# Attention before two MoE layers: products per head in tiles of 64 columns, a state per head without masks, and heads 6 and 7 moved by DMA

## The chip, the cores and the metric

The kernel runs on one core of a Trainium2 chip. The time is that of one execution on the device in microseconds; the number given for a kernel is the median of its runs. The core's engines are TensorE (PE, whose weight loads the trace lists apart as PEld), VectorE (DVE), ScalarE (ACT), GpSimd (POOL) and SyncE (SP), which issues all the DMAs spoken of here. Each engine works through its own instructions in the order of the program and waits on semaphores for the others.

## What is computed

Three layers in a row, all f32. The first is an attention with a decaying state, for 4 batch entries, 8 heads, 768 steps and 48 elements per head:

```python
state = np.zeros((B, H, D, D), dtype=np.float32)
for t in range(S):
    cur = np.einsum('bhd,bhe->bhde', u[None] * kt, vt)
    y[:, :, t] = np.einsum('bhd,bhde->bhe', rt, state + cur)
    state = w[None, :, :, None] * state + np.einsum('bhd,bhe->bhde', kt, vt)
```

Its output, 3072 tokens by 384, goes through a layer `x @ w_in`, the activation h * tanh(softplus(h)) and `@ w_out` with 2048 inner columns, and then through a mixture of 8 experts with 1024 inner columns each. The change concerns the attention alone, and the order of the rows of `w_in`.

## The kernel before

The attention is computed by chunks of 128 steps. A unit is one chunk c (of 6) of one batch entry b (of 4), with all 8 heads; the 24 units run with b as the inner loop, so that a unit's state is next needed four units later. Heads go in pairs: p counts 4 pairs, j the two heads of a pair. In tiles with head elements on the partitions (`ld`, `rt`, `kd`, the state) head j = 0 of a pair lies in partitions 0 to 47 and head j = 1 in 64 to 111; partitions 48 to 63 hold nothing of use.

For each unit PE makes the scores (`a_scores`, L614, 48 rows of 64 per product), DVE copies those below the diagonal over a matrix A into which ACT has put the diagonals (`a_tri`, L619, `a_diag`, L606), and PE makes the outputs `ya` (`a_out`): state times r (L653) and v times A (L655), both heads of a pair into the same 96 partitions. For that the state is a block-diagonal matrix of 112 by 96 for each pair, and v stands in `vz`, a copy padded with zeros, one for each j (`a_vz`, L572, ACT). The chunk's own contribution `un` (`a_kv`, L626, PE) is made for whole pairs, 112 by 96; ACT multiplies its two halves by a mask `hm`, so that the blocks between different heads become zero (`a_mask`, L636), and DVE adds it to the decayed state, pair by pair (`a_state`, L644). ACT moves `ya` out of PSUM into `xT`, the transposed activations of the next layer (`a_evac`): pairs 0 to 2 in one instruction (L664), pair 3, which is heads 6 and 7, in three pieces of 32 partitions into the rows 96 to 127 (L666). POOL and DVE prepare the diagonals (`a_q`, L582 and L583, `a_b`, L588), DVE scales k and r (`a_kh`, `a_kd`, `a_rt`). Every other iteration one weight tile of the next layer is converted on the side (`a_cv`: four DVE operations L142 to L157, an ACT copy, two POOL operations).

The order around this is written by hand. The tuple `steps` lists functions with an offset: in iteration i the function is called for unit i + offset, and each engine gets its instructions in that order. Each iteration thus mixes, for instance, the scores of unit i, the output of unit i - 1 and the loads of unit i + 2 (v) and i + 3 (k and r). Loads of v have two buffers, `ya` has one PSUM bank, `un` two that alternate, the scores three. In the last iterations the first token tile of the next layer is split into two parts (`split_x`) for its first matmuls. `stepwise_attention` is a second form of the same attention that runs only on inputs outside a tested range, after the whole of the first; it doesn't run here.

Of the kernel before, what the change touches and what calls it, by code (L numbers as in the profile page):

```python
# [9 lines left out]
F32 = mybir.dt.float32  # L10
# [11 lines left out]
NP = H // 2  # L22
DD = 2 * D
DR = 64 + D
C = 128
# [22 lines left out]
NVZ = 3  # L48
# [32 lines left out]
def layers(ctx: ExitStack, tc: tile.TileContext, a, out, bad, general):  # L81
# [388 lines left out]

    def chunked_attention(aw, ac):
# [4 lines left out]
        ld, lt, lv = {}, {}, {}  # L476

# [14 lines left out]
        hm = ac.tile([DR, 2], F32, name="hm")  # L492
        nc.sync.dma_start(hm, a["hmask"])
# [23 lines left out]
        vzs = []  # L517
        for i in range(NVZ):
            vz = wA.tile([128, NP, 2, DD], F32, name=f"vz{i}", tag="w")
            pool.memset(vz, 0.0)  # L520
            vzs.append(vz)

# [25 lines left out]
        def tables():  # L548
# [3 lines left out]
            for p in range(NP):  # L552
                tp = bank([128, 128], f"tp{p}", f"y{p % 3}")
# [76 lines left out]
        def a_mask(i):  # L630
            c, b = aunits[i]
            if c == NC - 1:
                return
# [4 lines left out]
            T[i]["um"] = um  # L638

        def a_state(i):  # L640
# [1044 lines left out]
```

## Time and profile before

| | us |
|---|---|
| median of 3 runs | 2027.22 |
| runs | 2024.59 to 2029.64 |
| the profiled execution | 2026.27 |
| its span, from the first to the last instruction | 2024.5 |

| engine | busy us in the span | share |
|---|---|---|
| PE | 1990.4 | 98% |
| DVE | 1360.1 | 67% |
| ACT | 1063.1 | 53% |
| POOL | 751.6 | 37% |

The attention is the first part of the span; its last output product begins at 151.0 us. In the timeline a row is a run of equal instructions: start, time from the start of the first to the end of the last, engine, line, operation, what is written and read, sizes, count, and in brackets how long the engine stood before and for whom. One f32 product of this attention appears as two MATMUL instructions. The end of a matmul is modelled, and matmuls overlap, so their starts say more than their lengths.

### The profile page before, as it was taken

The numbers are of one execution on the slowest core, as the hardware profiler recorded it, in microseconds if no ns is written. First come the engines' busy times: TensorE is split into PE (matmuls) and PEld (weight loads), VectorE is DVE, ScalarE is ACT, GpSimd is POOL, SyncE is SP. The second block draws the span as 40 slices with busy tenths as digits, with TensorE's granted clock in tenths as the row PEclk, the third lists the DMA queues.
The fourth block names the chain that finished last, engine by engine and source line by source line (L and its number), as shares of the span: only waits on it lengthen the run. The fifth ranks groups of instructions, "written<-read, shape, count | busy, mean of one in ns | idle before, by whom it ended". The sixth has DMA issues, their size and how long they took to land.

```text
span 2024.5 us, 27279 instructions
## 1 busy us (share of the span) xinstructions
PE 1990.4 (98%) x9334; PEld 1647.8 (81%) x9334; DVE 1360.1 (67%) x2177; ACT 1063.1 (53%) x2204; POOL 751.6 (37%) x639
## 2 busy tenths in 40 slices
PE   8899999999999999999999999999999999999998
PEld 7888888887778888877878888888888888888887
DVE  8998889778787777678764455555465555455554
ACT  7998888888755545444443433343344343333332
POOL 5546565557554333355561243311044011011110
PEclk8999999999999999999999999999999999999999
DMA  8750111010246655655465665558545566445440
GB/s 255 214 150 30 32 32 40 24 35 1 96 154 234 228 207 192 203 211 201 156 225 165 189 215 194 190 153 262 162 151 155 135 182 226 141 151 159 143 120 33
DMA packets 169156, 305.96 MB, mean 151 GB/s; under 512 B 39664, under 2 KB 85424, under 8 KB 169008
## 3 DMA queue, kind: packets, MB, share of 16 engines
q1 hardware_dynamic: 169008, 304.13, 46.7%
q8 instruction: 76, 1.25, 0.3%
q14 instruction: 72, 0.59, 0.1%
HBM read 226.90 MB, written 77.17 MB: 150 GB/s over the span
## 4 chain that ended last, share of the span: by engine, by line
PE 89%; DVE 5%; ACT 2%; issue 2%; POOL 1%; DMA 1%; DVEq 0%; SPq 0%; POOLq 0%; ACTq 0%
PE y L1039 37%; PE Bk L907 16%; PE U L907 15%; PE ph L246 9%; PE x L331 9%; ACT A L606 1%; PE ya L655 1%; DVE tc L939 1%; DVE A L619 1%; PE un L626 0%; DMA lv<-in_v_dram 0%; PE sc L614 0%; ACT xT L666 0%; DVE r L826 0%; PE ya L653 0%
## 5 line engine op out<-in xcount | busy, mean ns | idle before, releaser
L1039 PE MATMUL y<-gf,w 128*128 128x512 f32 x2088 | 570.4, 390 | 0.0
L1039 PEld LDWEIGHTS y<-gf,w 128*128 128x128 f32 x2088 | 391.0, 188 | 82.5 <-DVE gf L1031 1.5
L1039 PE MATMUL y<-ge,w 128*128 128x512 f32 x1368 | 373.8, 390 | 0.0
L1062 POOL TENSOR_TENSOR xT<-xT,xT 128x512 f32<-128x512 f32 x102 | 142.3, 1410 | 577.3 <-DVE xT L1061 576.0
L1029 ACT ACTIVATE gf<-tc 128x512 fp32r<-128x512 f32 x232 | 146.5, 632 | 389.6 <-DVE tc L939 375.6
L939 DVE TENSOR_TENSOR tc<-tc,Bk 128x512 f32<-128x512 f32 x270 | 185.1, 685 | 237.8 <-PE Bk L907 222.3
L939 DVE TENSOR_TENSOR tc<-tc,U 128x512 f32<-128x512 f32 x270 | 185.3, 686 | 222.7 <-PE U L907 208.3
L1039 PEld LDWEIGHTS y<-ge,w 128*128 128x128 f32 x1368 | 256.2, 188 | 53.5 <-DVE ge L1031 0.5
L1029 ACT ACTIVATE ge<-tc 128x512 fp32r<-128x512 f32 x152 | 96.1, 632 | 248.3 <-DVE tc L939 237.6
L331 PE MATMUL x<-g,wm 128*128 128x512 f32 x864 | 212.2, 390 | 0.3 <-POOL g L320 0.2
L246 PE MATMUL ph<-xs,wm 128*128 128x512 f32 x864 | 212.0, 390 | 0.3 <-POOL xs L216 0.3
L1031 DVE SCALAR_TENSOR_TENSOR gf<-tc,gf 128x512 fp32r<-128x512 f32 x232 | 193.5, 837 | 22.9 <-ACT gf L1029 18.2
L246 PEld LDWEIGHTS ph<-xs,wm 128*128 128x128 f32 x864 | 161.8, 188 | 36.5 <-POOL xs L216 0.7
L331 PEld LDWEIGHTS x<-g,wm 128*128 128x128 f32 x864 | 161.8, 188 | 35.2 <-DVE xT L347 0.8
L320 POOL TENSOR_TENSOR g<-y,g 128x512 fp32r<-128x512 f32 x96 | 125.0, 1302 | 102.2 <-ACT g L315 95.6
L937 ACT ACTIVATE tc<-Bk 128x512 f32<-128x512 f32 x192 | 114.3, 595 | 85.3 <-PE Bk L907 78.7
L937 ACT ACTIVATE tc<-U 128x512 f32<-128x512 f32 x192 | 114.4, 596 | 83.5 <-PE U L907 78.7
L907 PE MATMUL Bk<-xc,wc 128*128 128x512 f32 x540 | 152.0, 390 | 0.9 <-DVE tc L939 0.9
L907 PE MATMUL U<-xc,wc 128*128 128x512 f32 x540 | 151.7, 389 | 0.0
L1031 DVE SCALAR_TENSOR_TENSOR ge<-tc,ge 128x512 fp32r<-128x512 f32 x152 | 127.7, 841 | 21.4 <-ACT ge L1029 15.7
L847 POOL TENSOR_TENSOR w<-r,w 128x384 fp32r<-128x384 f32 x64 | 68.6, 1074 | 186.6 <-ACT w L846 175.4
L907 PEld LDWEIGHTS Bk<-xc,wc 128*128 128x128 f32 x540 | 101.1, 188 | 23.0 <-DVE tc L939 1.8
(256 smaller groups left out, 3210.9 us busy)
## 6 DMA issues: line engine op xcount, KB each, us to landing
wc<-keep SPq DMA_DIRECT2D x208, 384.0 KB, 3.7
w<-keep SPq DMA_DIRECT2D x128, 384.0 KB, 5.5
keep<-wc SPq DMA_DIRECT2D x104, 384.0 KB, 3.6
r<-in_w_dram SPq DMA_DIRECT2D x128, 192.0 KB, 3.7
keep<-w SPq DMA_DIRECT2D x64, 384.0 KB, 3.0
ld<-in_rkT_dram SPq DMA_DIRECT2D x24, 448.0 KB, 4.8
pb<-prow SPq DMA_DIRECT2D x42, 256.0 KB, 8.5
lt<-in_kr_dram SPq DMA_DIRECT2D x24, 384.0 KB, 5.1
```

Of the source, the lines that this page charges most:

```text
L246: pe.matmul(ph, w[:, pw, k, :], xs[:, px, :], start=(m == 0), stop=(m == 3 * KI - 1))
L320: pool.tensor_tensor(gs[i][:, 1], y, gs[i][:, 0].bitcast(F32), op=ALU.subtract)
L331: pe.matmul(sums[n][k], wo[f][:, pw, k, :], g[:, px, :], start=(f == f0 and m == 0), stop=(f == f1 and m == 1), skip_group_check=True)
L606: act.activation(A[:, h % 2, h // 2, :], ident, AF.Copy, scale=T[i]["bc"][:, h:h + 1])
L847: eng.tensor_tensor(flat(t[:, 1]), src, flat(t[:, 0]).bitcast(F32), op=ALU.subtract)
L907: pe.matmul(out_, w[:, pw, :], x[px], start=bool(start and m == 0), stop=bool(stop and m == 2), skip_group_check=True)
L937: act.activation(t, b, AF.Copy, scale=1.0 if kind == "c" else -1.0)
L939: dve.tensor_tensor(t, t, b, op=ALU.add if kind == "+" else ALU.subtract)
L1029: act.activation(g[:, 0], t, AF.Relu)
L1031: return lambda: dve.scalar_tensor_tensor(g[:, 1], t, 0.0, g[:, 0].bitcast(F32), op0=ALU.max, op1=ALU.subtract)
L1039: pe.matmul(Y[t][k], w[:, pw, k, :], x[:, px, :], start=(f % NF2 == 0 and m == 0), stop=(f % NF2 == NF2 - 1 and m == 2), skip_group_check= ...
L1062: pool.tensor_tensor(o, o, t_, op=ALU.add)
```

## The change

The two heads of a pair no longer share an output tile. `a_out` makes v times A for head j = 0 into partitions 0 to 47 and for j = 1 into 64 to 111, straight from the loaded v, and adds state times r to each with a product of 48 rows and 48 columns at the same place. So no padded copy of v is needed, and the state is one block of 48 columns per pair and head without blocks between heads: `a_kv` makes `un` by head, masks are gone. The decay of the state is one POOL multiplication (`a_decay`), the addition one DVE operation (`a_add`). `ya` is one PSUM tile for all units, cleared once. `a_evac` moves 112 partitions of pairs 0 to 2 into `xT` (row 48 to 63 and 112 to 127 of it hold nothing yet) and pair 3 into a staging tile `stg`, one for each token tile; after the last chunk of a token tile six DMAs (`spread_heads`) move heads 6 and 7 from there into those free rows, 16 partitions each. The rows of `w_in` are ordered accordingly on the host. v has four buffers in place of two, and `steps` has a new order.

```diff
+    def spread_heads(n, src):
+        for k in range(KI):
+            for j in range(2):
+                nc.sync.dma_start(xT[n][64 * j + D:64 * j + 64, k, :], src[64 * j + 16 * k:64 * j + 16 * k + 16])
...
+        lvs = [wA.tile([128, NP, 2, D], F32, name=f"lv{i}", tag="w") for i in range(4)]
+        stg = [wA.tile([128, TT], F32, name=f"stg{n}", tag="w") for n in range(NT)]
...
-            lv[i] = aw.tile([128, DM], F32, name=f"lv{i}", tag="lv")
+            lv[i] = lvs[i % 4]
...
+        ya = []
+
         def marks():
+            ya.append(bank([DR, NP, C], "ya", "y2"))
+            dve.memset(ya[0], 0.0)
...
-        st2 = [wA.tile([DR, 2, NP, DD], F32, name=f"st{b}", tag="w") for b in range(B // 2)]
-        st = [st2[b // 2][:, b % 2] for b in range(B)]
+        st = wA.tile([DR, B, NP, D], F32, name="st", tag="w")
...
-        def a_vz(i):
-            vz = vzs[i % NVZ]
-            vh = lv[i].rearrange("t (p j d) -> t p j d", p=NP, j=2)
-            for j in range(2):
-                act.activation(vz[:, :, j, j * D:(j + 1) * D], vh[:, :, j, :], AF.Copy)
-            T[i]["vz"] = vz
...
-            un = bank([DR, NP, DD], f"un{i}", f"y{i % 2}")
+            un = bank([DR, NP, D], f"un{i}", f"y{i % 2}")
+            kh = T[i]["kh"]
             for p in range(NP):
-                pe.matmul(un[:, p, :], T[i]["kh"][:, p].rearrange("t j d -> t (j d)")[:, 0:DR], lv[i][:, p * DD:(p + 1) * DD],
-                          start=True, stop=True)
+                pe.matmul(un[0:64, p, :], kh[:, p, 0, :], lv[i][:, p, 0, :], start=True, stop=True)
+                pe.matmul(un[64:DR, p, :], kh[:, p, 1, 0:D], lv[i][:, p, 1, :], start=True, stop=True)
...
-            um = st[b] if c == 0 else T[i]["un"]
-            for j in range(2):
-                act.activation(um[:, :, j * D:(j + 1) * D], T[i]["un"][:, :, j * D:(j + 1) * D], AF.Copy,
-                               scale=hm[:, j:j + 1])
...
+        def a_decay(i):
             c, b = aunits[i]
             if 0 < c < NC - 1:
-                for p in range(NP):
-                    dve.scalar_tensor_tensor(st[b][:, p, :], st[b][:, p, :], w128[:, p:p + 1], T[i]["um"][:, p, :],
-                                             op0=ALU.mult, op1=ALU.add)
+                pool.tensor_tensor(st[:, b], st[:, b], w128.unsqueeze(2).to_broadcast([DR, NP, D]), op=ALU.mult)
+
+        def a_add(i):
+            c, b = aunits[i]
+            if c == 0:
+                act.activation(st[:, b], T[i]["un"], AF.Copy)
+            elif c < NC - 1:
+                dve.tensor_tensor(st[:, b], st[:, b], T[i]["un"], op=ALU.add)
...
-            y = bank([DD, NP, C], f"ya{i}", "y2")
+            y = ya[0]
             for p in range(NP):
+                pe.matmul(y[0:D, p, :], lv[i][:, p, 0, :], x["A"][:, 0, p, :], start=True, stop=(c == 0))
+                pe.matmul(y[64:DR, p, :], lv[i][:, p, 1, :], x["A"][:, 1, p, :], start=True, stop=(c == 0))
                 if c > 0:
-                    pe.matmul(y[:, p, :], st[b][:, p, :], x["rt"][:, p, :], start=True, stop=False)
-                for j in range(2):
-                    pe.matmul(y[:, p, :], x["vz"][:, p, j, :], x["A"][:, j, p, :],
-                              start=(c == 0 and j == 0), stop=(j == 1))
+                    for j in range(2):
+                        r = slice(64 * j, 64 * j + D)
+                        pe.matmul(y[r, p, :], st[r, b, p, :], x["rt"][r, p, :], start=False, stop=True)
...
-            act.activation(xt[0:DD, :, x0:x0 + C], y[:, 0:KI, :], AF.Copy)
-            for k in range(KI):
-                act.activation(xt[DD:128, k, x0:x0 + C], y[32 * k:32 * k + 32, KI, :], AF.Copy)
+            n = blk // NSUB
+            act.activation(xt[0:DR, :, x0:x0 + C], y[:, 0:KI, :], AF.Copy)
+            act.activation(stg[n][0:DR, x0:x0 + C], y[:, KI, :], AF.Copy)
+            if i == ends[n]:
+                spread_heads(n, stg[n])
...
-        steps = ((load_d, 3), (a_tri, -1), (a_scores, 0), (a_kv, 0), (a_out, -1), (load_v, 2),
-                 (a_q, 1), (a_state, -2), (a_kh, 1), (a_evac, -2), (a_rt, 1), (a_diag, 0),
-                 (a_cv, 0), (a_mask, -1), (a_vz, 1), (a_kd, 1), (a_b, 1))
+        steps = ((load_d, 3), (a_tri, -1), (a_add, -2), (a_evac, -2), (a_scores, 0), (a_out, -1), (a_kv, 0),
+                 (a_q, 1), (a_kh, 1), (a_rt, 1), (a_diag, 0),
+                 (a_cv, 0), (a_kd, 1), (a_b, 1), (a_decay, -1), (load_v, 2))
```

On PE, at the end of the scores of one iteration in the middle of the attention: `sc` are the scores, `un` the unit's contribution to the state, `ya` the output; sizes are those of the result, partitions by columns. Before:

```order
L614 MATMUL sc_145<-rt_979,kd_1004 128x128
L614 MATMUL sc_144<-rt_979,kd_1004 128x128
L614 MATMUL sc_145<-rt_979,kd_1004 128x128
L626 MATMUL un_1022<-lv_898,kh_182 112x96 x4
L653 MATMUL ya_1027<-rt_912,st_188 96x128
L655 MATMUL ya_1027<-A_981,vz_153 96x128 x2
```

The last two rows stand there four times, once for each pair. Now the output comes right behind the scores, and `un` behind the output; this is the last pair of an output and the beginning of `un`:

```order
L648 MATMUL ya<-rt_482,st 48x128 x2
L643 MATMUL ya<-A_548,lv_110 48x128
L644 MATMUL ya<-A_548,lv_110 48x128
L648 MATMUL ya<-rt_482,st 48x128 x2
L622 MATMUL un_606<-lv_111,kh_182 64x48
L623 MATMUL un_606<-lv_111,kh_182 48x48
```

Twelve products of 96 partitions have become sixteen of 48, in which a pair's two products over 128 rows alternate with two over 48 rows, and four products `un` have become eight; PE's order of output and `un` is exchanged.

On DVE, the beginning of an iteration, with the copies by mask of unit i - 1, the state of unit i - 2 and the scaling of k and r of unit i + 1. Before:

```order
L619 COPY_PREDICATED A_914<-tri,sc_146 128x512
L619 COPY_PREDICATED A_914<-tri,sc_144 128x512
L644 SCALAR_TENSOR_TENSOR st_187<-st_187,w_186,un_805 112x96 x4
L599 TENSOR_TENSOR kh_182<-lt_793,Wkh 128x8x48
L593 TENSOR_TENSOR rt_979<-ld_791,Wr 112x512
```

Now:

```order
L614 COPY_PREDICATED A_686<-tri,sc_152 128x512
L614 COPY_PREDICATED A_686<-tri,sc_150 128x512
L636 TENSOR_TENSOR st<-st,un_606 112x192
L594 TENSOR_TENSOR kh_183<-lt_575,Wkh 128x8x48
L588 TENSOR_TENSOR rt_757<-ld_573,Wr 112x512
```

Four operations of 96 columns gave way to one of 192; the rest stands as it stood.

On POOL, over two iterations: the two products of `a_q` of each (`aq`), and the two operations of the weight conversion (`v`, `wm`) in one of them. Before:

```order
L582 TENSOR_TENSOR aq_758<-lt_584,ub 128x384
L583 TENSOR_TENSOR aq_758<-aq_758,lt_584 128x384
L171 TENSOR_TENSOR v_706<-v_706,wm_712 128x384
L176 TENSOR_TENSOR wm_712<-v_706,q_707 128x384
L582 TENSOR_TENSOR aq_825<-lt_651,ub 128x384
```

Now:

```order
L629 TENSOR_TENSOR st<-st,w_186 112x192
L577 TENSOR_TENSOR aq_753<-lt_575,ub 128x384
L578 TENSOR_TENSOR aq_753<-aq_753,lt_575 128x384
L170 TENSOR_TENSOR v_695<-v_695,wm_701 128x384
L175 TENSOR_TENSOR wm_701<-v_695,q_696 128x384
L629 TENSOR_TENSOR st<-st,w_186 112x192
```

The decay of the state stands at the end of each iteration, behind all else that POOL does in it.

## Rows read from the trace of the kernel before

**Rows 1.** Busy us (count): PE, PEld, DVE, ACT, POOL; clock; DMA share; GB/s
```profile
60.00:70.00 10.00, 9.31 (x93) 8.55 (x92) 9.90 (x24) 8.95 (x30) 5.72 (x6) 1.00 0.78 241
...
200.00:210.00 10.00, 10.00 (x46) 8.29 (x45) 9.79 (x14) 8.41 (x19) 7.42 (x6) 1.00 0.13 40
```

**Rows 2.** Timeline of DVE, two iterations: start us, us, instruction, count
```profile
56.31 1.33 DVE L619 COPY_PREDICATED A<-tri,sc 128x512 f32<-128x512 uint8 x2
...
57.54 0.97 DVE L644 SCALAR_TENSOR_TENSOR st<-st,w,un 112x96 f32<-112x96 f32 x4
58.44 0.55 DVE L599 TENSOR_TENSOR kh<-lt,Wkh 128x384 f32<-128x384 f32 x1
...
60.56 1.33 DVE L619 COPY_PREDICATED A<-tri,sc 128x512 f32<-128x512 uint8 x2
...
66.88 1.33 DVE L619 COPY_PREDICATED A<-tri,sc 128x512 f32<-128x512 uint8 x2
```

**Rows 3.** Timeline of DVE, copies by mask 14 iterations apart
```profile
44.16 1.35 DVE L619 COPY_PREDICATED A<-tri,sc 128x512 f32<-128x512 uint8 x2
...
123.99 1.33 DVE L619 COPY_PREDICATED A<-tri,sc 128x512 f32<-128x512 uint8 x2
```

**Rows 4.** Waits in 45 to 130 us: total us, times, longest
```profile
DVE st L644 <- PE ya L653: 1.6, 4, 0.5
DVE A L619 <- ACT A L606: 1.5, 3, 0.6
```

**Rows 5.** Timeline of PE, one iteration without a wait
```profile
85.48 1.16 PE L614 MATMUL sc<-rt,kd 48*128 48x128 f32 x16
86.57 1.02 PE L626 MATMUL un<-lv,kh 128*112 128x96 f32 x8
87.43 0.38 PE L653 MATMUL ya<-rt,st 112*96 112x128 f32 x2
...
89.63 0.60 PE L655 MATMUL ya<-A,vz 128*96 128x128 f32 x4
90.16 1.16 PE L614 MATMUL sc<-rt,kd 48*128 48x128 f32 x16
```

**Rows 6.** Timeline of ACT, one iteration without a weight conversion
```profile
126.22 2.45 ACT L606 ACTIVATE A<-ident,bc 128x128 f32<-128x128 f32 x8
128.69 0.82 ACT L636 ACTIVATE un<-un,hm 112x192 f32<-112x192 f32 x2
129.43 0.60 ACT L572 ACTIVATE vz<-lv 128x192 f32<-128x192 f32 x2
129.94 0.47 ACT L664 ACTIVATE xT<-ya 96x384 f32<-96x384 f32 x1
130.42 0.82 ACT L666 ACTIVATE xT<-ya 32x128 f32<-32x128 f32 x3
```

**Rows 7.** Groups of POOL, 45 to 130 us: busy us, mean ns, idle before
```profile
L582 POOL TENSOR_TENSOR aq<-lt,ub 128x384 f32<-128x384 f32 x12 | 13.0, 1082 | 10.5 <-DMA lt<-in_kr_dram 5.5 <-DVE A L619 2.6 <-DVE st L644 2.5
```

**Rows 8.** Timelines of ACT, then DVE, at the start, with waits
```profile
23.45 0.62 ACT L572 ACTIVATE vz<-lv 128x192 f32<-128x192 f32 x2 [2.96 <-DMA lv<-in_v_dram]
...
27.49 1.35 DVE L619 COPY_PREDICATED A<-tri,sc 128x512 f32<-128x512 uint8 x2 [1.46 <-ACT A L606]
```

**Rows 9.** Timeline of PE, products of 16 columns before products of 128
```profile
393.43 0.39 PE L383 MATMUL gp<-xg,wga 128*16 128x512 f32 x1
393.66 0.40 PE L384 MATMUL gp<-xg,wgb 128*16 128x512 f32 x1
393.89 2.21 PE L246 MATMUL ph<-xs,wm 128*128 128x512 f32 x9
```

**Rows 10.** Timeline of SP, one issue of a load
```profile
66.31 0.42 SPq L481 DMA_DIRECT2D ld<-in_rkT_dram  x1
```

**Rows 11.** PE at 80.2 us: busy, granted clock, DMA; then its timeline
```profile
80.20:80.40 0.20, 0.04 (x1) 0.50 1.02 328
...
80.36 1.78 PE L626 MATMUL un<-lv,kh 128*112 128x96 f32 x8 [0.37 <-issue]
```

More of the change, by code (lines that the diff above doesn't have):

```diff
@@ L47 @@
 NWA = 24
-NVZ = 3
 NG = 3
@@ L491, in chunked_attention @@
         nc.sync.dma_start(wT, a["wT"])
-        hm = ac.tile([DR, 2], F32, name="hm")
-        nc.sync.dma_start(hm, a["hmask"])
         load_d(0)
@@ L516, in chunked_attention @@
         pool.memset(warm, 0.0)
[L517 to L521, printed above, removed]
         wb = bank([128, 128], "wb", "y2")
@@ L552, in tables @@
             for p in range(NP):
-                tp = bank([128, 128], f"tp{p}", f"y{p % 3}")
+                tp = bank([128, 128], f"tp{p}", f"y{p % 2}")
                 pe.matmul(tp[:, 0:DR], Wh[:, p, :], ident[:DR, :DR], start=True, stop=True)
                 act.activation(Wkh[:, p], tp.rearrange("t (j d) -> t j d", j=2)[:, :, 0:D], AF.Copy)
+        ya = []
         def marks():
+            ya.append(bank([DR, NP, C], "ya", "y2"))
+            dve.memset(ya[0], 0.0)
             dve.tensor_copy(tri, trf.unsqueeze(1).to_broadcast([128, NP, 128]))
@@ L562, in marks @@
             dve.scalar_tensor_tensor(okw, wT, W_MAX, okw, op0=ALU.is_le, op1=ALU.mult)
-        st2 = [wA.tile([DR, 2, NP, DD], F32, name=f"st{b}", tag="w") for b in range(B // 2)]
-        st = [st2[b // 2][:, b % 2] for b in range(B)]
+        st = wA.tile([DR, B, NP, D], F32, name="st", tag="w")
         T = [{} for _ in aunits]
-        def a_vz(i):
-            vz = vzs[i % NVZ]
-            vh = lv[i].rearrange("t (p j d) -> t p j d", p=NP, j=2)
-            for j in range(2):
-                act.activation(vz[:, :, j, j * D:(j + 1) * D], vh[:, :, j, :], AF.Copy)
-            T[i]["vz"] = vz
+        ends = {(b * NC + c) // NSUB: i for i, (c, b) in enumerate(aunits)}
         def a_kd(i):
@@ L686, in chunked_attention @@
         a_q(0)
-        a_vz(0)
         for i in range(NA + 1):
@@ L711, in stepwise_attention @@
         nc.sync.dma_start(uT, a["uT"])
-        sel = ac.tile([DR, 3 * D - 1], F32, name="sel")
+        sel = ac.tile([DR, DR + D - 1], F32, name="sel")
         pool.memset(sel, 0.0)
         for j in range(2):
-            nc.sync.dma_start(sel[:, (j + 1) * D - 1:(j + 1) * D], a["hmask"][:, j:j + 1])
+            nc.sync.dma_start(sel[:, 64 * j + D - 1:64 * j + D], a["hmask"][:, j:j + 1])
         sts = [ac.tile([DR, S + 1], F32, name=f"sts{j}") for j in range(2)]
@@ L723, in stepwise_attention @@
         rk = ac.tile([DR, 2, NC, C], F32, name="rk")
+        stg = [wA.tile([128, TT], F32, name=f"stg{n}", tag="w") for n in range(NT)]
         for b in range(B):
@@ L728, in stepwise_attention @@
                 rT, kT = (rk[:, j].rearrange("d c t -> d (c t)") for j in range(2))
-                y = [bank([DD, S // 2], f"yg{b}_{p}_{g}", f"y{2 * (p % 2) + g}") for g in range(2)]
+                y = [bank([DR, S // 2], f"yg{b}_{p}_{g}", f"y{2 * (p % 2) + g}") for g in range(2)]
                 for e in range(D):
@@ L740, in stepwise_attention @@
                     for g in range(2):
-                        pe.matmul(y[g], sel[:, D - 1 - e:3 * D - 1 - e], x[:, g * S // 2:(g + 1) * S // 2],
+                        pe.matmul(y[g], sel[:, D - 1 - e:DR + D - 1 - e], x[:, g * S // 2:(g + 1) * S // 2],
                                   start=(e == 0), stop=(e == D - 1))
@@ L747, in stepwise_attention @@
                     if p < KI:
-                        act.activation(xt[0:DD, p, x0:x0 + C], yc, AF.Copy)
+                        act.activation(xt[0:DR, p, x0:x0 + C], yc, AF.Copy)
                     else:
-                        for k in range(KI):
-                            act.activation(xt[DD:128, k, x0:x0 + C], yc[32 * k:32 * k + 32, :], AF.Copy)
+                        act.activation(stg[blk // NSUB][0:DR, x0:x0 + C], yc, AF.Copy)
+        for n in range(NT):
+            spread_heads(n, stg[n])
     if general:
@@ L1659, in _lay_out @@
     p = np.arange(128)
-    perm = np.stack([np.where(p < DD, i * DD + p, 3 * DD + 32 * i + p - DD) for i in range(KI)])
+    j, d = p // 64, p % 64
+    perm = np.stack([np.where(d < D, i * DD + j * D + d, 3 * DD + j * D + 16 * i + d - D) for i in range(KI)])
     wi = np.asarray(x["moe_w_in"])[perm.reshape(-1)]
```

6 lines of the change are left out of this document (removed).

## The prediction

> **What bounds the kernel now.** I read the busy times in equal stretches first. From 200 to 210 us TensorE (PE) is busy 10.00 of 10 us [rows 1], with the matmuls of the first layer after attention: no edit of attention shortens that part, it can only start earlier or later. So the change is worth what it takes off the stretch before. There, between 60 and 70 us, VectorE (DVE) is busy 9.90 us and PE 9.31, with ScalarE (ACT) at 8.95 [rows 1]: three engines near full, so the next question is which one is last.
>
> The order in time on DVE answers it. One iteration of the loop handles one unit, a chunk of one batch entry, and I count it from one pair of copies by mask (L619) to the next: 56.31 to 60.56 is 4.25 us, 60.56 to 66.88 is 6.32 us, with no wait marked inside [rows 2]; the longer one, every other iteration, holds the four weight-conversion operations. The mean without gaps is (4.25 + 6.32)/2 = 5.29 us. Over the 14 iterations from 44.16 to 123.99 us it is 79.83/14 = 5.70 us [rows 3]. The missing 0.41 us is waits and stretched operations: in 45 to 130 us DVE waited 1.5 us for ACT's diagonals and 1.6 us for PE's reads of the state [rows 4]. PE needs, in an iteration without waits, 4.68 us (85.48 to 90.16) [rows 5], ACT 2.45 + 0.74 + 0.51 + 0.48 + 0.82, 5.0 us [rows 6]. So **DVE ends last, ACT is 0.3 us behind it, PE 0.6 us**.
>
> **The change, part by part.**
>
> *State update.* Four operations on DVE, 0.90 us (57.54 to 58.44) [rows 2], become one addition of 192 columns on DVE and one multiplication on POOL. No row shows the addition. The nearest, kh with 384 columns, takes 0.55 us [rows 2], so it lies between half of that and all of it; I take 0.30, near the half, since the width is what differs. DVE saves 0.60 us (0.35 to 0.63) in each of 16 units (batch entries times the four chunks that update): **9.6 us** (5.6 to 10.1). The multiplication on POOL costs by halves of L582's 1.08 us [rows 7] some 0.54 us, up to 1.08. POOL has room for that, but waits ahead of it for PE's output products, and the next a_q stands queued behind; its result is wanted at the far end of the next iteration, so that hides it. Without that cover DVE's reduction would wait the 2.2 us of a_q's two operations. A busier POOL can also stretch DVE's operations between buffers; I put 0.05 us an iteration on it, 0.8 in all (0 to 4).
>
> *ACT.* The masks (0.74), the zero-padded copies of v (0.51) and three small moves (0.82) go, one move like those (0.27) comes: 5.0 - 2.07 + 0.27, 3.2 us an iteration [rows 6]. ACT leaves the path. What it gives directly is DVE's wait for it, 1.5 us; its other effect falls on the start. There ACT stood 2.96 us for a load of v and DVE then 1.46 us for ACT [rows 8]; now only PE needs v. That gives 1.46 us, less a clearing of one PSUM bank on DVE at the start, which I bound by a mask copy, 0.65: **0.8 us net** (0 to 3).
>
> *PE.* One f32 product of 128 columns is two instructions 0.11 us apart (four in 0.60 us, two in 0.38) [rows 5]. The scores (L614) use 64 rows each: 16 instructions in 1.09 us, where one after the other they would need 1.76. So two halves of the rows run side by side, 8 x 0.11 = 0.88, and 0.21 is left; before them the last product would hand over at 90.07 (89.63 + 4 x 0.11) and they start at 90.16. That is 0.30 us for going to 64 rows and back, 0.15 a change of form. Before, an iteration has 2 such changes; after it has 10, because each pair p goes from 128 rows (v times A) to 64 (state times r) and back. The streams after: scores 0.88; v times A, 16 instructions on two column halves, 0.88 if these run side by side as the row halves do, 1.76 if not; state times r 0.88; the update un, 16 instructions of 48 columns where 8 of 96 took 0.86 [rows 5], between 0.43 and 0.86, taken as 0.50, since the columns are halved. With 10 x 0.15: 0.88 x 3 + 0.50 + 1.50 = **4.64 us**, as before, out of fewer columns and more changes. The bounds are 3.1 (changes free) and 5.9 (halves one by one: 0.88 + 1.76 + 0.88 + 0.86 + 1.50).
>
> Two rows speak of the form. Two products on 32 columns stand between products on 128 at 393.43 and 393.66, and the next begins at 393.89: steps of 0.23, no gap [rows 9], so columns alone cost nothing to change; rows did. The Trainium skill, "TensorEngine Tiling (Array Packing)", Key Properties, says that any change of tiling mode drains the engine, and these rows do not bear that out for columns. By the page the ten changes stay (4.64), by these rows alone they would go (3.1).
>
> No run here shows two column halves at once. The Trainium skill, "TensorE: Matmul & The Clock Gate", Part 3, says that column groups run concurrently, three of them 2.38 times as fast; by it the sum stays 4.64.
>
> DVE comes to 5.29 - 0.60 = 4.69 us and PE to 4.64: **a tie** where PE had 0.6 us to spare. DVE's iterations are alternately long and short, PE's equal, so in the short ones (3.65) DVE will wait for PE. I charge 0.15 us an iteration, 2.4 in all (0 to 8), and let half of the old waits of 3.1 us go (1.5).
>
> *Row moves.* 36 DMAs on SP, six for each of six token tiles, each some 0.42 us to issue [rows 10]. They wait for ACT's copy, and the loads of v and the next unit queue behind, but those are issued one to two iterations ahead; at most 2.5 us of issue stands in one iteration, against 4.7. The rows moved are first read in iterations 21 on, at the split of the first token tile, whose last part is ready in 14. Cost 0; without that cover a landing would show once, some 5 us.
>
> **The sum**: 9.6 + 1.5 + 0.8 - 2.4 - 0.8 = 8.7 us gained. The profiled execution took 2026.27 us (span 2024.5 and 1.8 around it), 0.95 below the median of 2027.22. 2026.3 - 8.7 = 2017.6, or **2018.5** beside the median.
>
> **Rivals.**
>
> *Column halves do not run side by side, slower.* Then PE needs 5.9 us; with the 0.41 of waits that DVE's bound had, 6.3 against 5.70, 16 x 0.59 = 9.4 lost, 0.8 back at the start: 2027.2 + 8.6, near 2036. It decides from 5.7 us of PE on. For it: no row shows columns side by side. Against: the rows' halves do so, to the last 0.11 us.
>
> *Nothing to be seen.* The change of form costs 0.25 us rather than 0.15 (blocks of four instructions refill each time), PE 5.6; or the clock. PE streams about 3.1 us of 5, with holes; at 80.2 us, after pauses, the granted clock was 0.50, the 1.2 GHz level, and the eight un instructions took 1.78 us in place of 1.02 [rows 5, 11]. With PE tied those 0.76 us fall on the path, and eleven more such stretches take the gain. Time: 2023 to 2031.
>
> *More is gained.* If the short loads of 48 columns make the changes cheap, PE needs under 4 us and DVE runs without waits: 9.6 + 3.1 + 1.5 - 0.4 = 13.8, that is 2013.
>
> **How the numbers follow.** Forecast (2015 to 2021) 0.44; more 0.15; nothing 0.24; slower by the halves 0.13, by other ends of the bounds (POOL's stretch, loads behind the moves) 0.04. About 0.3%, 6 us, is what a measurement here can tell from no change. So faster 0.58, same 0.25, slower 0.17. The range reaches from 2009 (5.70 - 4.69 us in all 16 iterations, no wait left, and 2 us at the start: 18 gained) to 2034, most of the way to the slower rival: below it lie 0.06, above 0.14.
>
> **What would show it.** DVE's copies by mask should come 5.1 us apart on average where they were 5.70, with one addition near 0.30 us behind them. PE's v times A of one pair should take 0.22 us (0.44: the slower rival), and out products some 3.0 us in all; if 2.3, the larger gain. ACT should show idle time of more than 1 us an iteration. The granted clock between 45 and 130 us tells the clock's part. The prediction is wrong if PE's iteration exceeds 5.2 us, or if DVE waits for POOL's multiplication.

## The result, and the profile after

The changed kernel takes 2054.44 us (median of 5 runs, 2053.77 to 2064.76) where the kernel before takes 2027.16 beside it (5 runs, 2024.59 to 2029.64): a ratio of 1.0145 (95% interval 1.0129 to 1.0161). It is **27 us slower** where 8.7 us less had been forecast; the time lies above the range, which ended at 2034. The profiled execution of after is the longest of the five, 2064.76 us with a span of 2062.9, and the account below is for that one: 38.4 us more than the span of before. The other four have a mean granted clock of 0.965 to 0.967 over the span where this one has 0.959; no profile shows where they differ.

All of it lies in the attention. Its last output product begins at 191.04 us, 40.0 us after that of before (151.0). What follows is as dense as it was [rows 1]. The stretches of after that answer to [rows 1], in the same columns (busy us and count of PE, PEld, DVE, ACT, POOL; then the granted clock of TensorE, DMA share, GB/s):

```profile
40.00:50.00 10.00, 10.00 (x81) 5.53 (x81) 8.08 (x15) 3.72 (x12) 4.56 (x5) 0.50 1.02 256
60.00:70.00 10.00, 10.00 (x90) 6.26 (x90) 4.84 (x9) 4.34 (x15) 5.93 (x7) 0.50 0.79 214
120.00:130.00 10.00, 10.00 (x82) 5.59 (x80) 6.47 (x12) 2.98 (x10) 4.62 (x5) 0.50 0.64 175
180.00:190.00 10.00, 10.00 (x54) 6.29 (x52) 1.17 (x6) 2.07 (x5) 3.01 (x3) 0.68 0.27 67
200.00:210.00 10.00, 9.41 (x41) 7.81 (x42) 9.86 (x16) 8.55 (x18) 8.13 (x7) 1.00 0.21 56
```

Read the PE column and the clock together. PE is busy 10.00 of 10 us, and DVE, which ended last before with 9.90, is down to 4.84. But the clock is **0.50**, the 1.2 GHz level, in every stretch of ten microseconds from 40 to 180; before, the stretch from 60 to 70 showed 1.00 [rows 1], and falls in the loop were short. The fall of [rows 11], to 0.50 at 80.2 us, was over at 83.6 us; PE's rows in it and behind it, the same four instructions:

```profile
82.36 1.06 PE L655 MATMUL ya<-A,vz 128*96 128x128 f32 x4
...
84.29 0.60 PE L655 MATMUL ya<-A,vz 128*96 128x128 f32 x4
```

The timeline of PE in one iteration, which answers to [rows 5] (start, length, line, operation, sizes, count):

```profile
61.74 2.08 PE L609 MATMUL sc<-rt,kd 48*128 48x128 f32 x16
63.75 0.45 PE L643 MATMUL ya<-A,lv 128*48 128x128 f32 x1
63.76 0.45 PE L644 MATMUL ya<-A,lv 128*48 128x128 f32 x1
...
64.35 0.67 PE L648 MATMUL ya<-rt,st 48*48 48x128 f32 x4
64.94 0.45 PE L643 MATMUL ya<-A,lv 128*48 128x128 f32 x1
...
68.53 0.34 PE L622 MATMUL un<-lv,kh 128*64 128x48 f32 x1
...
69.54 2.08 PE L609 MATMUL sc<-rt,kd 48*128 48x128 f32 x16
```

An iteration takes 69.54 - 61.74 = 7.80 us; the forecast was 4.64. The scores take 2.01 us here (1.09 in [rows 5]) and a pair 64.94 - 63.75 = 1.19. The pair's four steps of 0.213 us (25.74 to 25.95, below) make 0.85 of that, so its two changes of form cost 0.17 each, some 1.7 us of the 7.80 for all ten. The column of busy time doesn't show these gaps, since the end of a product is modelled. From one pair of copies by mask on DVE to the second after it are 15.60 us, 7.80 an iteration, where [rows 3] gave 5.70. About 18 iterations with 2.1 us more each are the 38 us. DVE's own rows, which answer to [rows 2], show the engine waiting:

```profile
64.34 1.32 DVE L614 COPY_PREDICATED A<-tri,sc 128x512 f32<-128x512 uint8 x2
69.23 0.35 DVE L636 TENSOR_TENSOR st<-st,un 112x192 f32<-112x192 f32 x1 [3.56 <-POOL st L629]
...
79.94 1.32 DVE L614 COPY_PREDICATED A<-tri,sc 128x512 f32<-128x512 uint8 x2
```

And the waits of after, 45 to 170 us, which answer to [rows 4] (engine and line, for whom it waited: total us, times, longest):

```profile
ACT xT L657 <- PE ya L648: 70.2, 17, 4.8
POOL st L629 <- PE ya L648: 68.0, 16, 8.4
DVE st L636 <- POOL st L629: 41.3, 16, 4.0
```

DVE waits for POOL, but POOL for PE's output products, as ACT does: three engines stand behind one. The place where the clock falls is in the timeline of PE too. In the chunk without a state, where an output is v times A alone, PE works at 0.50 first (25.74 to 25.95: 0.21 us a step), and the clock rises at 29.3 us, while PE streams (29.94 to 30.16: two steps in 0.22). Then PE pauses for DVE (the brackets: how long, for whom), and the clock falls at 36.1 us, 1.6 us after PE had begun again, so that a step takes 0.22 us from 36.30 on and the next scores 2.73:

```profile
25.74 0.42 PE L643 MATMUL ya<-A,lv 128*48 128x128 f32 x1
...
25.95 0.42 PE L643 MATMUL ya<-A,lv 128*48 128x128 f32 x1
...
29.94 0.27 PE L643 MATMUL ya<-A,lv 128*48 128x128 f32 x1
29.95 0.27 PE L644 MATMUL ya<-A,lv 128*48 128x128 f32 x1
...
30.16 0.27 PE L643 MATMUL ya<-A,lv 128*48 128x128 f32 x1
...
33.35 0.49 PE L609 MATMUL sc<-rt,kd 48*128 48x128 f32 x2 [2.02 <-DVE kd L572]
34.45 1.16 PE L609 MATMUL sc<-rt,kd 48*128 48x128 f32 x14 [0.61 <-DVE A L614]
...
36.30 0.42 PE L643 MATMUL ya<-A,lv 128*48 128x128 f32 x1
...
36.52 0.42 PE L643 MATMUL ya<-A,lv 128*48 128x128 f32 x1
...
37.70 2.73 PE L609 MATMUL sc<-rt,kd 48*128 48x128 f32 x16
```

Before, the clock also fell after pauses, and came back. Here it comes back at 186 us only, in the first layer's products of 128 by 512, which begin at 182.47. The Trainium skill, "TensorE: Matmul & The Clock Gate", section "Why this matters for your kernels", lays such drops to gaps in which TensorE is idle. The fall at 36.1 us fits that in so far as pauses of 2.02 and 0.61 us stand ahead of it; that the clock stayed at 0.50, with PE busy 10.00 of 10 us from 40 to 190, the rule does not explain.

### The profile page after: what moved, and what is told of

Same layout as the page of the kernel before. It is cut to its first block, busy times and chain, and to the rows that moved or that the text cites. A ratio compares the mean times of both kernels' runs of the same rounds, so it can differ in the third digit from the quotient of the medians.

```text
span 2062.9 us, 27802 instructions
## 1 busy us (share of the span) xinstructions
PE 2037.0 (99%) x9654; PEld 1641.1 (80%) x9654; DVE 1354.4 (66%) x2130; ACT 1021.3 (50%) x2072; POOL 760.3 (37%) x652
## 4 chain that ended last, share of the span: by engine, by line
PE 94%; DVE 3%; issue 1%; DMA 1%; POOL 1%; ACT 0%; SPq 0%; DVEq 0%; POOLq 0%; ACTq 0%
PE y L1034 36%; PE Bk L902 15%; PE U L902 15%; PE ph L245 10%; PE x L330 9%; PE ya L643 2%; PE ya L648 2%; PE sc L609 2%; PE un L622 1%; DVE tc L934 1%; DVE r L821 0%; DMA lt<-in_kr_dram 0%; DMA wc<-keep 0%; PE un L623 0%; DVE sw L821 0%
## 5 line engine op out<-in xcount | busy, mean ns | idle before, releaser
L1026 DVE SCALAR_TENSOR_TENSOR gf<-tc,gf 128x512 fp32r<-128x512 f32 x232 | 194.6, 841 | 22.7 <-ACT gf L1024 17.9
```

What stands on the lines that cost most here:

```text
L1026: return lambda: dve.scalar_tensor_tensor(g[:, 1], t, 0.0, g[:, 0].bitcast(F32), op0=ALU.max, op1=ALU.subtract)
```

## The experiments

**Theory:** the changed kernel's work is what was forecast, and the granted clock alone makes it slow. **Rivals:** the changes of form cost more than forecast; or the wait for POOL's multiplication holds the loop up. All kernels below start from the changed one. Each time stands beside runs of the kernel before on the same chip; PE's iteration is read from scores to scores, without waits.

| kernel | us (median) | ratio to before | interval | clock at 60 to 70 us | PE's iteration |
|---|---|---|---|---|---|
| the change | 2054.44 | 1.0145 | 1.0129 to 1.0161 | 0.50 | 7.80 |
| e1_grouped | 2031.77 | 1.0027 | 1.0016 to 1.0038 | 0.66 | 3.9 at clock 1.00, from output to output |
| e2_state_whole | 2069.43 | 1.0211 | 1.0181 to 1.0240 | 0.50 | 8.21 |
| e3_va_whole | 2031.42 | 1.0016 | 0.9990 to 1.0042 | 1.00 | 5.53 |
| e4_filler4 | 2026.54 | 1.0001 | 0.9990 to 1.0013 | 1.00 | 5.61 |
| e10_fill4_small | 2096.31 | 1.0347 | 1.0326 to 1.0368 | 0.50 | 9.50 |
| e7_fill4_all | 2022.54 | 0.9985 | 0.9976 to 0.9995 | 1.00 | as e4_filler4 |
| e5_grouped_fill2 | 2017.90 | 0.9969 | 0.9953 to 0.9984 | 1.00 | DVE ends last |
| e6_grouped_fill4 | 2026.61 | 1.0010 | 0.9993 to 1.0028 | 1.00 | ties with DVE |
| e11_grouped_fill40 | 2020.38 | 0.9976 | 0.9965 to 0.9987 | 1.00 | DVE ends last |
| e9_grouped_fill42 | 2015.57 | 0.9940 | 0.9922 to 0.9958 | 1.00 | DVE ends last |
| **e12_grouped_fill424** | **2011.97** | **0.9925** | 0.9912 to 0.9939 | 1.00 | DVE ends last |

e8_fill1 had two executions, at 2074.95 and 2027.04 us, and stands below.

### Work thrown away, to see the clock

```diff
-            un = bank([DR, NP, D], f"un{i}", f"y{i % 2}")
+            ub_ = bank([128, 512], f"un{i}", f"y{i % 2}")
+            un = ub_[0:DR, 0:NP * D].rearrange("d (p e) -> d p e", p=NP)
+            for _ in range(4):
+                pe.matmul(ub_[:, 256:384], warm, warm, start=True, stop=True, skip_group_check=True)
```

> The changed kernel with four products of 128 by 128 by 128 on zeros ahead of un in every iteration but the last chunk's, into columns of un's bank that nothing uses. They are work that is thrown away, 0.86 us an iteration at 2.4 GHz, 1.7 at 1.2. Theory A: PE is given enough to do, the granted clock rises, the iteration falls from 7.80 to some 5.2 us and the time to 2015 to 2025 us although PE does more. Theory B: the clock is as it is, the iteration grows to 9.5 us and the time by 20 x 1.7 to near 2088 us.

It took 2026.54 us, 1.5 above theory A's range and 61 below theory B: PE got 1.09 us more to do in each iteration, and the kernel became 28 us faster. Its stretches, in the columns as above:

```profile
60.00:70.00 10.00, 10.00 (x125) 6.62 (x125) 9.73 (x17) 5.35 (x18) 6.04 (x7) 1.00 0.82 223
...
140.00:150.00 10.00, 10.00 (x48) 5.88 (x45) 1.34 (x2) 3.58 (x12) 3.21 (x3) 0.50 0.28 75
```

The clock is 1.00 from 30 to 130 us, and 0.50 again at 140 to 150, in the last chunk, which has no `un` and so none of the added products. One iteration of PE in it:

```profile
59.87 1.16 PE L609 MATMUL sc<-rt,kd 48*128 48x128 f32 x16
60.97 0.31 PE L646 MATMUL ya<-A,lv 128*48 128x128 f32 x1
...
61.67 0.31 PE L646 MATMUL ya<-A,lv 128*48 128x128 f32 x1
...
63.80 1.16 PE L622 MATMUL un<-warm 128*128 128x128 f32 x8
64.89 0.26 PE L625 MATMUL un<-lv,kh 128*64 128x48 f32 x1
...
65.48 0.76 PE L609 MATMUL sc<-rt,kd 48*128 48x128 f32 x8
```

Scores 1.10, outputs 2.83 (60.97 to 63.80), `un` 0.59 and the added products 1.09: 5.61 us, and **4.52 without the addition**, where 4.64 had been forecast. So the changed kernel's work is as large as forecast, and it is the clock that made 7.80 of it. The rival by POOL falls too: the multiplication stands where it stood, and DVE waits 3.5 us in all for it (45 to 130 us) where it waited 41.3 (45 to 170).

Is it any longer stretch of products that lifts the clock, or products that fill the array? The same four, on 48 rows and 48 columns:

```diff
-                pe.matmul(ub_[:, 256:384], warm, warm, start=True, stop=True, skip_group_check=True)
+                pe.matmul(ub_[0:D, 256:384], warm[0:D, 0:D], warm[0:D, :], start=True, stop=True, skip_group_check=True)
```

> As e4_filler4 (the changed kernel's own order, four thrown-away products ahead of un, none in the last chunk), but each of 48 rows by 48 columns of the array in place of 128 by 128; the streams are as long, 128 columns of data in two passes. Theory (the clock follows how much of the array works): these products lift nothing, the clock is 0.50 from 40 to 180 us, PE's iteration is about 7.80 + 4 x 0.43 + a change of form, 9.6 us, and the time is 2075 to 2095. Rival (any longer stretch of products without a change of form lifts the clock): 1.00 from 40 to 130 us as in e4_filler4 and 2025 to 2030.

```profile
60.00:70.00 10.00, 10.00 (x78) 6.71 (x75) 5.56 (x11) 3.57 (x12) 2.48 (x4) 0.50 0.28 79
```

2096.31 us, 1.3 above what the theory expected, and 0.50 from 20 to 210 us. Streams of the same length lift nothing here when they use a small tile: 70 us lie between the two kernels, and the size of four products is the only difference in the program.

With one whole product in place of four:

```diff
-            for _ in range(4):
+            for _ in range(1):
```

> The changed kernel in its own order with one thrown-away product in each iteration (none in the last chunk), where e4_filler4 has four. It tells how much work it takes. If the clock goes by the share of full-width streaming in a smooth way, one quarter of the work gives a mixed clock, 0.6 to 0.8 between 45 and 130 us, and a time of 2035 to 2048. If any full product in the loop is enough, the clock is 1.00 and the time 3 us below e4_filler4 (16 iterations with 0.82 us less, less what DVE then ends last), 2016 to 2024. If it is too little, 0.50 throughout and 2055 to 2060.

None of the three came. The same program took 2074.95 us in one execution, with a mean granted clock of 0.958 over the span, and 2027.04 in the other, with 0.990. The profile is of the first:

```profile
60.00:70.00 10.00, 10.00 (x78) 5.72 (x78) 5.52 (x9) 2.98 (x10) 4.74 (x5) 0.50 0.86 240
```

It shows 0.50 in every stretch from 40 to 190 us. Two executions say no more than that both occur.

Four products in the last chunk's units too:

```diff
-            if aunits[i][0] == NC - 1:
-                return
             ub_ = bank([128, 512], f"un{i}", f"y{i % 2}")
...
                 pe.matmul(ub_[:, 256:384], warm, warm, start=True, stop=True, skip_group_check=True)
+            if aunits[i][0] == NC - 1:
+                return
```

> The changed kernel in its own order with four thrown-away products in every iteration, where e4_filler4 left them out in the last chunk and the clock fell to 0.50 at 140 to 150 us. Theory: the clock stays 1.00 to the end of attention, the four units of the last chunk take 5.1 us each in place of about 8, and the time is 2016 to 2023. Rival (the clock falls there for another cause, the end of the other work on PE): 0.50 at 140 to 150 stays and the time is e4_filler4's 2026.5 or 4 us more.

2022.54 us, inside the theory's bounds, 4.0 less than e4_filler4, with the clock at 1.00 from 40 us to the end of attention.

### Changes of form, and which products matter

All v times A first, then all state times r, so that six of ten changes of form go:

```diff
-                pe.matmul(y[0:D, p, :], lv[i][:, p, 0, :], x["A"][:, 0, p, :], start=True, stop=(c == 0))
+                pe.matmul(y[0:D, p, :], lv[i][:, p, 0, :], x["A"][:, 0, p, :], start=(p == 0), stop=(c == 0 and p == NP - 1),
+                          skip_group_check=True)
...
+            for p in range(NP):
                 if c > 0:
                     for j in range(2):
```

> The changed kernel with the output's products in another order: v times A of all four pairs first, then state times r of all four, so that PE changes between 128 and 64 rows 4 times an iteration and not 10 times. Theory A, the clock: PE's iteration is 7.80 us because the granted clock stays at 0.50 from 40 to 185 us although PE is never idle; what counts is what PE is given to do. Theory B, the changes of form: they cost 0.17 us each at that clock (a pair takes 1.195 us, its streams 4 x 0.213). By B alone the clock stays at 0.50 and the iteration falls by 6 x 0.17 to 6.8 us, some 2034 us in all. By A it stays near 7 us unless the denser streams lift the clock; if they do, the iteration is under 5.2 us and the time near 2015 us.

2031.77 us, 22.7 less than the change, between what the two theories said and nearer to theory B's 2034. Where the clock is 1.00, PE's timeline reads:

```profile
48.36 0.31 PE L643 MATMUL ya<-A,lv 128*48 128x128 f32 x1
...
49.37 1.08 PE L651 MATMUL ya<-rt,st 48*48 48x128 f32 x16
50.38 0.26 PE L622 MATMUL un<-lv,kh 128*64 128x48 f32 x1
```

The outputs take 50.38 - 48.36 = 2.02 us, where e4_filler4's took 2.83: 0.81 for six changes, **0.135 us a change**; the forecast had 0.15. At the change's clock six changes are 1.0 us an iteration, so the time alone would fit theory B. But theory B left the clock at 0.50, and it is mixed (1.00 at 40 to 60, then 0.66 to 0.84 in all stretches to 130). Here it comes back by itself. PE pauses for DVE as in the change, the clock falls at 62.9 us, and it is back at 69.7 us, with nothing but the loop's own products between:

```profile
62.06 0.48 PE L609 MATMUL sc<-rt,kd 48*128 48x128 f32 x2 [1.07 <-DVE kd L572]
63.17 2.07 PE L609 MATMUL sc<-rt,kd 48*128 48x128 f32 x14 [0.62 <-DVE A L614]
...
69.85 1.16 PE L609 MATMUL sc<-rt,kd 48*128 48x128 f32 x16
```

From 60 to 142 us the clock falls seven times, and each time it is back after 3 to 7 us. The products are the change's own, of the same number and sizes; only their order differs, four changes of form an iteration in place of ten. So the change's products, in this order, do bring the clock back: the changes of form, which the rival counted by their price alone, have a part in whether it returns, as the size of the products has. The grouped order with the clock held is e5_grouped_fill2, below.

State times r as one product of 112 by 112 for each pair; the heads' values are mixed by it:

```diff
-                    for j in range(2):
-                        r = slice(64 * j, 64 * j + D)
-                        pe.matmul(y[r, p, :], st[r, b, p, :], x["rt"][r, p, :], start=False, stop=True)
+                    pe.matmul(y[:, p, :], st[:, b].rearrange("d p e -> d (p e)")[:, 16 * p:16 * p + DR],
+                              x["rt"][:, p, :], start=False, stop=(p == NP - 1), skip_group_check=True)
```

> The changed kernel with state times r as one product of 112 rows and 112 columns per pair in place of two of 48 by 48 (values of several heads are mixed, the output is not the attention's). The streams are as long as before (8 steps of 128 columns an iteration), the whole array works in them, and the only changes of rows left are those into and out of the scores. Theory A (the clock follows how much of the array works): the granted clock rises to 1.00 in most of 45 to 130 us, iteration near 5 us, 2010 to 2020 us. Theory B (changes of form): clock stays 0.50, iteration 7.80 - 8 x 0.17 = 6.4 us, near 2026 us.

```profile
62.73 0.42 PE L643 MATMUL ya<-A,lv 128*48 128x128 f32 x1
...
63.09 0.77 PE L648 MATMUL ya<-rt,st 112*112 112x128 f32 x2
63.79 0.45 PE L643 MATMUL ya<-A,lv 128*48 128x128 f32 x1
```

2069.43 us, at 0.50 from 40 to 180 us: neither theory came (2010 to 2020, or near 2026). Two things follow. Here both kinds of product use more than 64 rows and only the columns change, from 48 to 112, yet the step from 62.73 to 63.09 is 0.36 us, where products of one form stand 0.21 apart at this clock (25.74 and 25.95 in the timeline of after). **A change of columns alone costs about 0.15 us at 1.2 GHz**, and 0.28 on the way back (63.09 to 63.79 is 0.70, two steps of 0.21 and the change), so theory B's eight saved changes were not saved, and the iteration grew to 8.21 us. [Rows 9] had seemed to deny such a cost: the Trainium skill, "TensorEngine Tiling (Array Packing)", Key Properties, is right here. The steps of 0.23 us in [rows 9] stand as read; what I drew from them doesn't hold for these short streams. And larger products at this place don't lift the clock while the changes of form stay.

v times A with both heads' 96 columns, one after another; here too values are mixed:

```diff
-                pe.matmul(y[0:D, p, :], lv[i][:, p, 0, :], x["A"][:, 0, p, :], start=True, stop=(c == 0))
-                pe.matmul(y[64:DR, p, :], lv[i][:, p, 1, :], x["A"][:, 1, p, :], start=True, stop=(c == 0))
+                for j in range(2):
+                    pe.matmul(y[0:DD, p, :], lv[i][:, p].rearrange("t j d -> t (j d)"), x["A"][:, j, p, :],
+                              start=(j == 0), stop=(c == 0 and j == 1), skip_group_check=True)
```

> The changed kernel with v times A as products of 96 columns, one after the other, as wide as in the kernel before (values of both heads are mixed), state times r in its 48 by 48 tiles. Theory A: if it is the narrow column halves that leave the clock down, it rises to 1.00 and the iteration is 4.3 + 0.9 = 5.2 us or a little more, near 2022 us; if it is the 64-row tiles, it stays at 0.50 and the iteration is 7.80 + 1.7 = 9.5 us, near 2085 us. Theory B: changes stay, 9.5 us and near 2085 us.

```profile
60.00:70.00 10.00, 10.00 (x119) 7.47 (x116) 8.45 (x17) 6.48 (x21) 6.13 (x8) 1.00 0.78 218
```

2031.42 us, 9 above theory A's 2022, with the clock at 1.00 from 40 to 130 and PE's iteration at 5.53 (61.72 to 67.25) where 5.2 had been expected. PE has 1.0 us more to do than the change (5.53 against 4.52 at the full clock) and needs 2.3 us less. So it is enough to take back one part of the change, the two narrow products side by side in place of the two wide ones, and the clock is there again, though PE changes form as often as in the change.

### The grouped order with the clock held

The order of e1_grouped, and two thrown-away products in every iteration, the last chunk's too:

```diff
-            for _ in range(4):
+            for _ in range(2):
```

> The output products in the order of e1_grouped, and in every iteration, those of the last chunk too, two products of 128 rows by 128 columns on zeros, thrown away, ahead of un. Theory (the granted clock, not the work, made the changed kernel slow): the clock stays near 1.00 from 45 to 150 us, PE needs about 3.8 + 2 x 0.27 = 4.35 us an iteration, DVE ends last with the 4.97 us that e1_grouped showed where its clock was 1.00, and the whole comes to 2008 to 2018 us. Rival (fewer changes of form are what helped e1_grouped, the clock is a matter of its own): the clock stays mixed as in e1_grouped, 0.5 to 1.0, and the time is 2028 to 2036, e1_grouped's 2031.8 with the added work on top.

2017.90 us. The rival, by which e1_grouped gained from fewer changes alone, would have had 2028 to 2036. DVE ends last again, as before the change. Where PE pauses for it, the clock still falls for a stretch (0.83 at 100 to 110 us; it is back at 106.5). The pause in PE's timeline, with the wait in brackets:

```profile
100.59 0.49 PE L609 MATMUL sc<-rt,kd 48*128 48x128 f32 x2 [0.46 <-DVE kd L572]
101.70 1.16 PE L609 MATMUL sc<-rt,kd 48*128 48x128 f32 x14 [0.62 <-DVE A L614]
```

Four in every iteration:

```diff
-            for _ in range(2):
+            for _ in range(4):
```

> As e5_grouped_fill2 with four thrown-away products in place of two. PE needs about 3.8 + 4 x 0.27 = 4.9 us an iteration, which ties with DVE's 4.97. Theory: clock 1.00 as in e5_grouped_fill2, and a time 0 to 8 us above it, since PE now has no spare time. If two products are too few to hold the clock and four are enough, this one is the faster by 5 to 15 us.

2026.61 us, a miss: 8.7 above e5_grouped_fill2 (forecast 0 to 8). PE and DVE tie, pauses come as well, and the clock was 0.83 to 0.85 in three stretches between 80 and 120 us and 0.63 to 0.69 from 130 to 150. So more thrown-away work wasn't better here. Whether it matters that it stands where PE would wait is the question of the next two.

Four in the odd iterations, which hold the weight conversion on DVE, and two in the even ones, or none (`else 0`):

```diff
-            for _ in range(2):
+            for _ in range(4 if i % 2 else 2):
```

> As e5_grouped_fill2, but four thrown-away products in the odd iterations, after which PE waited for DVE in e5_grouped_fill2 (0.46 and 0.62 us at 100.59 and 101.70) and its clock fell to 0.50 for a stretch, and two in the even ones. Theory: PE needs 9.25 us for a pair of iterations where DVE needs 9.57, so it still isn't last; the pauses shrink, the clock falls less often between 80 and 130 us, and the time is 2010 to 2018. Rival (the pauses have nothing to do with it): as e5_grouped_fill2 or up to 3 us more.

> As e9_grouped_fill42, without the two products in the even iterations: the same number of products as in e5_grouped_fill2, all of them in front of the pause. If only the pauses matter, it is like e9_grouped_fill42 or 1 to 2 us below; if the clock goes by the work in every stretch, the even iterations let it fall, as in e1_grouped, and the time is 2020 to 2032.

e9_grouped_fill42 took 2015.57 us and showed 0.98 to 1.00 from 40 to 120 us, as its theory had it; its times (2010.51 to 2018.24) and those of e5_grouped_fill2 (2013.90 to 2022.92) overlap, so that they alone don't tell the two kernels apart. DVE's copies by mask are 9.57 us apart for two iterations:

```profile
53.96 1.34 DVE L614 COPY_PREDICATED A<-tri,sc 128x512 f32<-128x512 uint8 x2
...
63.53 1.34 DVE L614 COPY_PREDICATED A<-tri,sc 128x512 f32<-128x512 uint8 x2
```

e11_grouped_fill40 took 2020.38 and does not tell the two cases apart: its time is at the edge of the second one's bounds, but its clock was 1.00 from 30 to 100 us, as in the first. Last, four in all units of the last chunk as well:

```diff
-            for _ in range(4 if i % 2 else 2):
+            for _ in range(4 if i % 2 or aunits[i][0] == NC - 1 else 2):
```

> As e9_grouped_fill42, but four thrown-away products in all four units of the last chunk, where e9_grouped_fill42 had the clock at 0.62 from 120 to 130 and 0.53 from 130 to 140 us, after PE had waited 1.46 and 0.62 us for DVE. Theory: the clock comes back sooner or doesn't fall there, 5 us at most are saved, and the time is 2010 to 2016. Rival (a pause that long lowers the clock whatever follows): as e9_grouped_fill42, 2015 to 2018.

```profile
60.00:70.00 10.00, 10.00 (x152) 8.41 (x146) 9.90 (x19) 6.61 (x22) 7.47 (x8) 1.00 1.04 266
...
120.00:130.00 10.00, 8.31 (x82) 6.81 (x81) 9.82 (x17) 6.73 (x21) 5.58 (x5) 0.83 0.31 87
130.00:140.00 10.00, 10.00 (x95) 8.14 (x94) 2.85 (x9) 4.11 (x11) 3.25 (x3) 1.00 0.32 78
```

2011.97 us (2011.28 to 2014.00), 15.6 below the kernel before beside it (2027.53): the lowest median of all, though its interval overlaps that of e9_grouped_fill42. It is the change with its outputs grouped and 2 to 4 products thrown away. In the last chunk, from 130 to 140 us, its clock is 1.00 where e9_grouped_fill42's was 0.53. From 60 to 70 us it has DVE at 9.90, as [rows 1] had, but each iteration is shorter.

## Why the prediction was wrong, point by point

**The step that failed is the clock.** The prediction had it as a rival, in "Nothing to be seen": 0.76 us for one stretch at 0.50 after a pause, and "eleven more such stretches take the gain", 2023 to 2031. The mechanism was named and its size was taken from the wrong kind of event. [Rows 11] show a fall out of which PE came by its own products, some 3 us later; it was priced as if the products after the change would bring the clock back in the same way. They did not: the fall at 36.1 us lasted until 186 us. The term is not 8 us of single stretches but 7.80 - 4.52 = 3.28 us in each of some 18 iterations, 59 us, of which 21 are paid by what the change saves (5.70 - 4.52 an iteration) and 38 are left; this counts PE alone, and with the clock held DVE would end last, so that both parts are some 5 us too large. e4_filler4, e7_fill4_all and e10_fill4_small show that it is the clock; e3_va_whole and e1_grouped show two ways to have it back, wide products v times A, or the same products with six changes of form fewer. The ten changes of form thus had a second price beside the 0.15 us each that the sum gave them. The sentence in the prediction that should have warned is its own: PE streams "about 3.1 us of 5, with holes". It led to a price for holes and not to the question of whether PE would ever be granted the full clock there.

**PE's sum was right at the full clock.** 4.52 us against 4.64 (e4_filler4), and 2.83 for the output products where some 3.0 had been listed (4.78 in the change itself, 63.75 to 68.53). The column halves run side by side, 0.01 us apart (29.94 and 29.95), so the slower rival (2036) was wrong; the four instructions of one pair of heads take the 0.22 us that was listed (29.94 to 30.16). A change of form costs 0.135 us where 0.15 was taken. Only the sentence on [rows 9] was wrong, by which changes of columns alone would be free (e2_state_whole); the sum did not use it.

**State update: right.** The addition took 0.355 us in after and 0.34 in e9_grouped_fill42 (0.30 taken, 0.28 to 0.55), POOL's multiplication 0.507 us (0.54 taken). DVE waited 41.3 us in all for it, which had been listed as a sign of a wrong prediction, but POOL itself waited 68.0 us for PE; with the clock held DVE waited 3.5 us in e4_filler4 (45 to 130 us) and once, 0.7 us, in e9_grouped_fill42 (45 to 120 us). It was a consequence.

**ACT: right.** Its three remaining steps run from 60.84 to 63.83 us, 3.0 us (3.2 forecast, with a conversion copy of 0.52 every other iteration), and it then stands idle for PE:

```profile
60.84 0.49 ACT L657 ACTIVATE xT<-ya 112x384 f32<-112x384 f32 x1 [3.65 <-PE ya L648]
...
61.39 2.44 ACT L601 ACTIVATE A<-ident,bc 128x128 f32<-128x128 f32 x8
```

At the start, DVE's wait of 1.46 us for ACT [rows 8] is gone, and the third pair of copies by mask begins at 26.64 us where [rows 8] had 27.49: 0.85 earlier, 0.8 forecast. The agreement is partly luck: the second pair comes 1.44 us later than before (22.73 and 21.29), and the fourth and fifth are 0.36 earlier (33.68 and 34.04, 37.59 and 37.95).

**The tie: not measured.** No kernel here has the change's own order at the full clock without added products. With the outputs grouped, the clock at 1.00 and DVE last, e9_grouped_fill42's iteration is 9.57/2 = 4.79 us, near DVE's bare 4.69; the forecast had 5.1, with 0.15 for the tie and the old waits, but there PE has more room than the tie would leave. The nearest to a tie is e6_grouped_fill4, 8.7 us above e5_grouped_fill2, with falls of the clock. That points to a second price, which the prediction did not see: after a pause of PE the clock can fall, as it did at 36.1 us here and in e1_grouped.

**Row moves and contention.** No wait for the moved rows stands among the waits of after (160 to 205 us) or of e5_grouped_fill2 (40 to 205 us). No experiment took the moves away, so their cost of 0 is read from the trace and not tested; in e4_filler4 one wait of 0.8 us and in e3_va_whole one of 0.9 us are put down to them. The operations of DVE that read between buffers were no longer than before where the clock was held (kh 628 ns on average in e9_grouped_fill42, 734 before) and longer in the change itself (893).

The forecast of 2018.5 us lies near 2017.90 of e5_grouped_fill2, but that is luck: e5_grouped_fill2 has six changes of form fewer and two products more in an iteration. The change's own order with the clock held is e7_fill4_all, 2022.54 us, with 1.09 us an iteration of added work in it.

**What stays open.** Which property of the products decides. Filling the array fits e3_va_whole, e4_filler4 and e10_fill4_small, but e2_state_whole, with larger products in place of small ones, stayed at 0.50, and e1_grouped, with products of the same sizes, came back. The gaps at the changes of form fit e1_grouped, e2_state_whole and the chunk without a state, where the clock rose at 29.3 us, but not e3_va_whole and e4_filler4, which have as many of them or more. No experiment here separates the two. Nor was it tried whether the kernel before could be held at 0.50, or why its own falls end.

## What to carry to other kernels

When a change packs small products side by side and alternates their forms, TensorE may lose its clock for as long as the loop lasts, though its rows show it busy throughout, as here; ask of every such loop not only how long its streams are but what would bring the granted clock back after its first pause, and read busy time and clock in the same row. If the clock has gone, a few whole-array products, even thrown away, are a cheap test and can be a cheap cure: 1.09 us of them per iteration bought 28 us here. Group products of one form: that bought 22.7 us by itself, and the clock came back after each fall. The fastest kernels here had DVE, not TensorE, end last, with few pauses of TensorE.

## What was not expected of the hardware

- TensorE stood at the 1.2 GHz level for some 150 us (36.1 to 186) while its rows from 40 on show it busy 10.00 of 10 us; with four more products of 128 by 128 by 128 in an iteration of 5.61 us it stood at 2.4 (e4_filler4), with four of 48 by 48 by 128 it did not (e10_fill4_small).
- The same products in another order, with four changes of form an iteration in place of ten, brought the clock back by themselves, 3 to 7 us after each of seven falls (e1_grouped).
- With one product of 128 by 128 by 128 (e8_fill1) the same program ran once at a mean clock of 0.958 (2074.95 us) and once at 0.990 (2027.04 us).
- A change of columns alone took 0.15 us at 1.2 GHz (0.36 against 0.21 between starts) and 0.28 on the way back; changes of rows and columns took 0.135 us each at 2.4 GHz.
- Two column halves on 128 rows start 0.01 us apart and run fully side by side: two steps of both take 0.22 us (29.94 to 30.16).
